# Other prices for float32 matmuls in a planned kernel, and constant matmuls in TensorE's planned gaps

## The chip, the cores and the metric

The kernel runs on one core of a Trainium2 chip. The metric is the device time of one execution in microseconds (us); less is better. Engines are called as in the profile: PE is TensorE (PEld its weight loads), DVE is VectorE, ACT is ScalarE, POOL is GpSimd, SP is SyncE, which here issues all DMAs.

## What is computed

An attention with random features, and behind it a feed-forward network (FFN) on its output, all in float32 to the outside:

```python
def phi(x):                                   # batch 8, heads 8, seq 576, head_dim 64, 128 features
    proj = np.einsum('bhsd,md->bhsm', x, omega)
    h = proj - np.sum(x * x, axis=-1, keepdims=True) / 2.0
    return np.exp(h - np.max(h, axis=-1, keepdims=True)) / np.sqrt(m)
q_p, k_p = phi(q * scale), phi(k * scale)
kv = np.einsum('bhsm,bhsd->bhmd', k_p, v)
num = np.einsum('bhsm,bhmd->bhsd', q_p, kv)
den = np.einsum('bhsm,bhm->bhs', q_p, np.sum(k_p, axis=2))[..., None] + 1e-06
x = (num / den).transpose(0, 2, 1, 3).reshape(4608, 512)
h = x @ w_in                                  # 512 x 2048
out = np.maximum(0.01 * h, h) @ w_out         # 2048 x 512
```

## The kernel before

The 4608 tokens are taken in nine blocks j of 512. For each block the attention is worked out for four pairs of heads (hp), and then the FFN of that block runs on PE. Key batches (`key_batch`, eight of them) deliver the sums over keys that a block needs; `query_block` does a block's queries. Batches 0 and 1 of the keys and block 0 of the queries are done in float32 (`Whole`): the projection at L636 (16 matmuls for four tiles of tokens, 4 more for a fifth tile), the sums over keys at L739, the transposes at L827 (`turn`) and the products with the sums at L856 (`num32`). All others (`Unit`) split each operand into two f16 parts: L572 projects, L751 to L753 sum over keys, L849 to L851 are the products. A block's products, divided (L866, L867, L869), are its x; x is split into f16 parts (`turned_parts`) and transposed by a DMA at L784 into the tiles `fix_xt`, on which the FFN works.

The FFN multiplies f16 parts in groups of 12 matmuls: L1210 up and L1234 down, with 512 columns, in the first blocks; L1126 and L1056, with 256 columns, where Strassen-like products are used. Block 0 has 16 groups up and 16 down. The weights arrive as eight pieces each of w_in and w_out (`fix_big`, SP L429 and L431), are converted (ACT L444 and L462, DVE L446, L449, L467, POOL L464), get the column sums of L457 on PE, and are split (L491, L335 and ACT L329) once their largest sum is known.

Nothing of this runs in the order in which it is written. Each step is an operation with one or more engines, a price in us for each, what it reads and writes, and a priority. `Plan.order` goes through time with these prices, gives each operation an engine and a start, gives each buffer a place, and so fixes the order on every engine, SP's queue included; then the operations are issued in that order, and each engine runs its own in order. FFN groups have the last priority, so they fill what the attention leaves of PE. `HOP` is the planned delay between an operation and its followers on other engines. The prices that the change touches are `PJ32` (0.5 us for a tile of tokens at L636), 10 x 0.235 at L739, 4 x 0.28 at L827 and 4 x 0.26 at L856.

PSUM, while the attention runs: three banks `ffn` (one of which first holds the column sums of the weights), two tiles `pj` for projections, one bank `mi` for everything small, so each product at L856 or L849 waits until the one before it has been read by L869.

Of the kernel before, what the change touches and what calls it, by code (L numbers as in the profile page):

```python
# [17 lines left out]
P = 128  # L18
# [38 lines left out]

UP_FIELD = 202 << 23
OM_DOWN = 2.0 ** 38
PJ, PJ32 = 0.07, 0.5  # L60


class Buf:
# [10 lines left out]
class Plan:  # L74
# [49 lines left out]
    def order(self):  # L124
# [44 lines left out]
        while len(done) < len(self.ops):  # L169
# [24 lines left out]
            for b in o.bufs:  # L194
                if b.place is None:
                    fs, us = place_free[b.kind], place_user[b.kind]
                    b.place = min((i for i in range(len(us)) if us[i] is None and (i < first_late[b.kind] or not early_left)),
                                  key=lambda i: fs[i])
                    us[b.place] = b
                    b.last, held_by[b.kind, b.place] = held_by.get((b.kind, b.place)), b  # L200
                    next_buf[b.kind] += 1
            o.start, o.engine = t, e
# [21 lines left out]
            for x in after[o.number]:  # L224
                x.waits -= 1
                x.ready = max(x.ready, t + o.cost if e == "PE" and "PE" in x.ways else end)
                if not x.waits:
                    open_.append(x)
        return done


def key_tiles(b):
# [26 lines left out]
def performer_ffn(ctx: ExitStack, tc, qT, kT, qn, kn, vn, omT, eye, w_in, w_out, out):  # L259
# [55 lines left out]
    def op(engine, cost, run, port=False, **of):  # L315
        return ways([(engine, cost, run, port or engine == "POOL")], **of)
# [393 lines left out]
    def key_batch(b, prio):  # L710
# [6 lines left out]
        for hp in range(HP):  # L717
# [14 lines left out]
            if b < WHOLE:  # L732
                def sums(u=u, edge=edge, acc=acc, hp=hp, parts=parts):
                    for j in range(2):
                        o = at(acc)[:, (2 * (hp % 2) + j) * E:(2 * (hp % 2) + j + 1) * E]
                        for t in range(VT):
                            c = t - b % 2
                            p = u.p()[:, 4 * j + c] if 0 <= c < 4 else edge32(edge)[:, j]
                            nc.tensor.matmul(o, p, parts()[:, hp, t, j], start=(t == 0), stop=(t == VT - 1))  # L739
                op("PE", 10 * 0.235, sums, r=[u.ph, edge, (v, 0), (v, 1)], w=[acc], prio=prio,  # L740
                   slack=1.0)
            else:
                def sums(u=u, edge=edge, acc=acc, hp=hp, parts=parts):
# [62 lines left out]
    def query_block(j, prio):  # L806

        for hp in range(HP):
# [6 lines left out]
            if j:  # L815

                for i in range(2):
                    op("SP", 1.25, lambda u=u, qp=qp, i=i: nc.sync.dma_start(out=at(qp)[:, i],
                       in_=flat(at(u.ph)[:, i]), transpose=True), r=[(u.ph, i)], w=[(qp, i)], prio=prio, moved=1 << 18)
            else:  # L820
                qp32 = lambda qp=qp: at(qp).rearrange("p a b t -> p (a b t)").bitcast(F32)
                for i in range(2):
                    turned = buf("ffn")

                    def turn(u=u, turned=turned, i=i):
                        for g in range(4):
                            nc.tensor.transpose(at(turned)[:, g * P:(g + 1) * P], u.p()[:, 4 * (g % 2) + 2 * i + g // 2, :],  # L827
                                                ident)
                    op("PE", 4 * 0.28, turn, r=[u.ph, "ident"], w=[turned], prio=prio)
                    high(512, lambda qp32=qp32, i=i: qp32()[:, 512 * i:512 * i + 512], lambda turned=turned: at(turned),  # L830
                         psum=True, r=[turned], w=[(qp, i)], prio=prio)
            strassen = j >= FIRST_S
# [2 lines left out]
            for i in range(2):  # L835
# [22 lines left out]
                if j:  # L858
                    op("PE", 12 * 0.035 + 0.1, num, r=[(qp, 0), (qp, 1), *((kvs[b], hp | 1) for b in used)], w=[acc],
                       prio=prio, slack=1.0)  # L860
                else:
                    op("PE", 4 * 0.26, num32, r=[(qp, i), (kvs["32"], hp | 1)], w=[acc], prio=prio)
                av = lambda acc=acc: at(acc)[:, :4 * E].rearrange("p (g e) -> p g e", e=E)

                def inverse(av=av, r=r, down=down):
# [399 lines left out]
    for j in range(NB):  # L1265
# [6 lines left out]
        if j + 1 < NB:  # L1272
# [3 lines left out]
                parts.append(key_batch(done_k, 0.0))  # L1276
            in_turn(*parts, query_block(j + 1, 0.0))
    order = plan.order()
    tiles.update({**opened(attention, "att", early, False), **opened(attention, "attps", early_banks, True)})
    ctx.push(attention)  # L1280
    opened_late = False
    with tc.manual_schedule():
        for o in order:
            if not opened_late and any(b.place >= len(tiles[b.kind]) for b in o.bufs):
                later()
                opened_late = True
            o.run()


# [45 lines left out]
```

## Time and profile before

| | us |
|---|---|
| median of 3 runs (lowest, highest) | 948.97 (947.88, 950.0) |
| the profiled execution | 958.32 |
| its span, from first to last instruction | 956.5 |
| busy: PE, DVE, ACT, POOL | 904.8, 707.7, 587.0, 419.7 |
| mean granted clock of PE | 0.967 |
| first FFN matmul (L1210) | 90.05 |

The lines are read so: a row of a stretch or a group gives busy time and, behind x, the number of instructions; idle time stands with what ended it. A float32 matmul of the program shows as two matmuls in the profile for L636, L739, L856 and L360, and as one for L827. PE's busy time holds the overlap of pipelined matmuls, so the price of one is read from the distance of starts.

### The profile page before, as it was taken

Reading aid. Unit: us, or ns where it says so; the run is one execution under the profiler, and the core shown is the slowest. Engines: PE = TensorE matmul, PEld = TensorE weight load, DVE = VectorE, ACT = ScalarE, POOL = GpSimd, SP = SyncE. Lnnn points to the kernel's source line nnn. Section 1 sums busy time; section 2 is a strip of 40 time slices with the busy share of each in tenths; the row PEclk is TensorE's granted clock in tenths of the full one; section 3 lists DMA queues with packets and bytes.
Section 4 is the critical chain, followed back from the end, with each engine's and each line's share of the span. In section 5 each row is a group of like instructions: output and inputs, shape, how many; then the busy total and the mean of one; then the engine's idle time right before and its main releaser. Section 6 shows DMA issues by size and latency. Waiting matters only on the chain.

```text
span 956.5 us, 20558 instructions
## 1 busy us (share of the span) xinstructions
PE 904.8 (95%) x8286; PEld 598.0 (63%) x8286; DVE 707.7 (74%) x1266; ACT 587.0 (61%) x874; POOL 419.7 (44%) x381
## 2 busy tenths in 40 slices
PE   4786999999999999998999999998998999999998
PEld 3785464645555545587557855784576647855887
DVE  7888987897899852887888777877786721285774
ACT  5777686557774763687747865786466723632661
POOL 2333541446665764336223640355025631555562
PEclk7786999999999999999999999999999999999999
DMA  9774446675587667898868995788779962751401
GB/s 368 256 210 126 142 112 148 149 159 121 99 137 186 138 166 175 172 199 226 219 142 186 238 243 126 180 201 187 159 123 209 227 123 82 201 130 40 133 1 45
DMA packets 260607, 155.07 MB, mean 162 GB/s; under 512 B 191648, under 2 KB 237472, under 8 KB 259488
## 3 DMA queue, kind: packets, MB, share of 16 engines
q1 hardware_dynamic: 260512, 153.76, 65.9%
q8 instruction: 65, 1.06, 0.5%
q14 instruction: 30, 0.25, 0.1%
HBM read 90.54 MB, written 16.78 MB: 112 GB/s over the span
## 4 chain that ended last, share of the span: by engine, by line
PE 79%; DMA 8%; DVE 8%; ACT 2%; issue 2%; SPq 1%; POOL 0%; DVEq 0%; ACTq 0%
PE fixps_ffn L1234 27%; PE fixps_ffn L1126 15%; PE fixps_ffn L1210 13%; DMA att_t<-att_z 5%; PE attps_pj L572 5%; PE lateps_ffn L1234 3%; PE attps_pj L636 3%; PE lateps_ffn L1056 3%; PE lateps_ffn L1126 2%; DMA att_qp<-att_ph 2%; PE fixps_ffn L1056 1%; PE attps_mi L849 1%; PE attps_mi L739 1%; DMA fix_xt<-fix_xn 1%; PE attps_mi L851 1%
## 5 line engine op out<-in xcount | busy, mean ns | idle before, releaser
L1234 PE MATMUL fixps_ffn<-fix_wt,fix_big 128*128 128x512 f16 x1392 | 314.3, 381 | 0.0
L1234 PEld LDWEIGHTS <-fix_big 128*128 128x128 f16 x1536 | 146.1, 98 | 168.2 <-issue 2.2
L335 POOL TENSOR_TENSOR fix_big<-fix_row,fix_big 128x512 f16<-128x512 f32 x131 | 162.3, 1246 | 201.4 <-ACT fix_big L329 191.4
L1126 PEld LDWEIGHTS <-fix_wt 128*128 128x128 f16 x2016 | 195.2, 98 | 29.7 <-issue 4.1
L1126 PE MATMUL fixps_ffn<-fix_xt,fix_wt 128*128 128x256 f16 x1800 | 208.1, 274 | 3.2 <-ACT fix_row L329 3.2
L1210 PE MATMUL fixps_ffn<-fix_xt,fix_wt 128*128 128x512 f16 x576 | 133.1, 386 | 2.1 <-DMA fix_xt<-fix_xn 2.1
L335 POOL TENSOR_TENSOR fix_xn<-fix_x,fix_xn 128x512 f16<-128x512 f32 (+1 forms) x36 | 42.3, 1174 | 129.7 <-ACT fix_xn L329 127.2
L1210 PEld LDWEIGHTS <-fix_wt 128*128 128x128 f16 x576 | 55.1, 99 | 66.5 <-issue 6.2
L591 ACT ACTIVATE att_p<-att_p,shift 128x1024 f32<-128x1024 f32 x68 | 69.7, 1028 | 40.4 <-DVE att_p L588 40.3
L329 ACT ACTIVATE fix_big<-fix_row 128x512 f16<-128x512 f32 x140 | 85.5, 623 | 10.6 <-DVE fix_wt L449 3.9
L579 DVE TENSOR_REDUCE att_st<-attps_pj 128x8 f32<-128x1024 f32 x68 | 72.8, 1076 | 19.3 <-PE attps_pj L572 19.3
L335 DVE TENSOR_TENSOR att_ph<-att_p,att_ph 128x1024 f16<-128x1024 f32 x56 | 75.6, 1355 | 10.4 <-ACT att_ph L329 10.3
L588 DVE SCALAR_TENSOR_TENSOR att_p<-attps_pj,att_sc,att_st 128x1024 f32<-128x1024 f32 x68 | 76.6, 1132 | 0.4
L1141 DVE TENSOR_TENSOR fix_row<-fix_row,fixps_ffn 128x512 f32<-128x512 f32 x64 | 43.9, 686 | 43.1 <-PE fixps_ffn L1126 21.7
L572 PE MATMUL attps_pj<-om,att_t 64*128 64x128 f16 x1416 | 51.1, 219 | 10.5 <-DMA att_t<-att_z 10.0
L329 ACT ACTIVATE att_ph<-att_p 128x1024 f16<-128x1024 f32 x55 | 57.5, 1047 | 1.4 <-PE attps_mi L753 1.1
L572 PEld LDWEIGHTS <-att_t 64*128 64x128 f16 x1416 | 40.5, 95 | 28.1 <-issue 14.1
L530 ACT ACTIVATE att_z<-att_nat 128x512 f32<-128x512 f32 (+1 forms) x56 | 36.2, 647 | 32.3 <-DMA att_t<-att_z 22.4
L532 DVE TENSOR_REDUCE att_sq<-att_z 128x8 f32<-128x512 f32 (+1 forms) x56 | 39.7, 708 | 21.4 <-ACT att_z L530 21.3
L1149 ACT ACTIVATE fix_row<-fix_row 128x512 f32<-128x512 f32 x70 | 43.5, 624 | 12.8 <-DVE fix_row L1141 12.4
L329 ACT ACTIVATE att_z<-att_nat,att_sc 128x512 f16<-128x512 f32 (+1 forms) x52 | 38.3, 739 | 21.0 <-DVE att_sc L542 21.0
L556 DVE SCALAR_TENSOR_TENSOR att_z<-att_nat,att_sc,att_z 128x512 f16<-128x512 f32 (+1 forms) x52 | 48.8, 941 | 3.2 <-ACT att_z L329 3.2
(185 smaller groups left out, 1584.4 us busy)
## 6 DMA issues: line engine op xcount, KB each, us to landing
fix_wt<-w1s SPq DMA_DIRECT2D x48, 512.0 KB, 4.7
fix_wt<-w1s SPq DMA_DIRECT2D x48, 384.0 KB, 3.9
att_v<-vn SPq DMA_DIRECT2D x16, 650.0 KB, 5.0
out<-fix_row SPq DMA_DIRECT2D x35, 256.0 KB, 2.3
fix_big<-w_in SPq DMA_DIRECT2D x8, 1024.0 KB, 10.1
fix_big<-w_out SPq DMA_DIRECT2D x8, 1024.0 KB, 5.4
att_nat<-qn SPq DMA_DIRECT2D x32, 256.0 KB, 3.3
w1s<-fix_y SPq DMA_DIRECT2D x32, 128.0 KB, 2.9
```

Source lines behind the costliest of these rows:

```text
L329: ("ACT", act(n, int(pointer)), lambda: nc.scalar.activation(dst(), src(), AF.Copy, scale=1.0 if scale is None else value()), False),
L335: return ways([(e, c, lambda g=g: g.tensor_tensor(dst(), a(), b(), op=ALU.subtract), True) for e, c, g in (("POOL", pool_(n), nc.gpsimd), ...
L556: op("DVE", stt(n) + 0.15, lambda: nc.vector.scalar_tensor_tensor(zl(), heads(), up(), zh(), op0=ALU.mult, op1=ALU.subtract), port=True, r ...
L572: nc.tensor.matmul(at(pj)[:, 512 * h + c * M:512 * h + (c + 1) * M], at(self.t)[r, 2 * (c0 + c) + x, :], om[r, w, :], start=(x + w == 0), ...
L579: op("DVE", dve(n * M), lambda: nc.vector.tensor_reduce(row(0), pv(), axis=AX.X, op=ALU.max), r=[pj], w=[st], prio=prio)
L588: op("DVE", dve(n * M), lambda: nc.vector.scalar_tensor_tensor(p(), pv(), down(), row(2).rearrange("p (g o) -> p g o", o=1).broadcast_to([ ...
L591: op("ACT", act(n * M, 1), lambda: nc.scalar.activation(flat(p()), flat(p()), AF.Exp, bias=shift), w=[p32], r=["ones"], prio=prio)
L1126: nc.tensor.matmul(o, unit(at(wb[c]), u)[:, wp, P * a:P * a + P], mixes[j, c][n][1](xp), start=(first and a == 0 and i == 0), stop=(a == 1 ...
L1141: op("DVE", dve(512), lambda: nc.vector.tensor_tensor(at(g), at(g), at(b), op=ALU.add), r=[b], w=[g], prio=top - 1.0)
L1149: op("ACT", act(512), lambda: nc.scalar.activation(at(g), at(src), AF.Prelu, scale=H_DOWN_D if finish else H_DOWN_S, alpha=0.01), r=[src], ...
L1210: nc.tensor.matmul(at(ph), wk[wp][:, c:c + P], xt[:, xp, :], start=(i == 0), stop=(i == 3 * KT - 1))
L1234: nc.tensor.matmul(at(po), part(f, gp)[:, t * P:(t + 1) * P], wf[wp], start=(f == 0 and gp == wp), stop=(f == FT - 1 and gp == 1))
```

## The change

Four prices of the planner are changed. And a function `between` goes through the order once it is fixed: wherever PE's next operation is planned at least 0.4 us behind the end of the one before, and one of the next 12 operations of PE is the first to write a `pj` or `ffn` buffer whose place is free by then, it notes a number of matmuls for that place, so many as take 0.8 of the gap at 256 columns / 2350 per us. When the kernel is issued, `busy` puts these in: `ident` (the 128x128 identity in float32, read as f16) is weight and operand, and the result goes into the PSUM place that the later operation will write over.

```diff
-PJ, PJ32 = 0.07, 0.5
+PJ, PJ32 = 0.07, 0.43
+FILL_FROM, FILL_LESS, FILL_SHARE, FILL_N = 0.4, 0.1, 0.8, 256
...
+                    b.free_at = fs[b.place]
...
+def between(order):
+    place = {o: i for i, o in enumerate(order)}
+    pe = [o for o in order if o.engine == "PE"]
+    first = [next((b for b in o.bufs if b.kind in ("pj", "ffn") and b.ops[0] is o), None) for o in pe]
+    fill, end = {}, pe[0].start + pe[0].cost
+    for i, o in enumerate(pe[1:], 1):
+        begin, gap = end, o.start - end
+        end = o.start + o.cost
+        if gap < FILL_FROM:
+            continue
+        for x, b in zip(pe[i:i + 12], first[i:i + 12]):
+            if b is None or (b.last and any(place[y] > place[o] for y in b.last.ops)):
+                continue
+            n = int((o.start - max(begin, b.free_at) - FILL_LESS) * FILL_SHARE / (FILL_N / 2350))
+            if n > 0:
+                fill[o] = b, n
+                break
+    return fill
...
-                op("PE", 10 * 0.235, sums, r=[u.ph, edge, (v, 0), (v, 1)], w=[acc], prio=prio,
+                op("PE", 10 * 0.118, sums, r=[u.ph, edge, (v, 0), (v, 1)], w=[acc], prio=prio,
...
-                    op("PE", 4 * 0.28, turn, r=[u.ph, "ident"], w=[turned], prio=prio)
+                    op("PE", 4 * 0.115, turn, r=[u.ph, "ident"], w=[turned], prio=prio)
...
-                    op("PE", 4 * 0.26, num32, r=[(qp, i), (kvs["32"], hp | 1)], w=[acc], prio=prio)
+                    op("PE", 4 * 0.118, num32, r=[(qp, i), (kvs["32"], hp | 1)], w=[acc], prio=prio)
...
     order = plan.order()
+    fill = between(order)
+    constant = ident.bitcast(F16)
+
+    def busy(b, n):
+        for _ in range(n):
+            nc.tensor.matmul(at(b)[:, :FILL_N], constant[:, :P], constant[:, :FILL_N], start=True, stop=True,
+                             skip_group_check=True)
...
+            if o in fill:
+                busy(*fill[o])
             o.run()
```

Lines of the changed kernel lie lower in the file by 25 from the projections on: L636 becomes L661, L739 L764, L827 L852, L856 L881, L457 L482, L1210 L1235, L615 L640, L429 L454. The fill is L1310. There are 412 fill matmuls, each with a weight load, in 30 runs of 2 to 40. Of them 321, in 24 runs, stand ahead of the first FFN matmul: 78 of these ahead of the first projection (in runs of 38, 35 and 5), the last ones in runs of 26, 15, 3 and 40. Three runs of 31, 24 and 17, and one of 2, stand where the first FFN block gives way to the second; runs of 6 and 11 come later.

Because the prices changed, all of the order is new. Three places show it. First, SP's queue at the start, where `fix_big` takes the pieces of w_in and `att_nat` the keys. Before:

```order
L380 DMA fix_xt_98<-omT 128x256
L381 DMA ident<-eye 128x128
L615 DMA att_nat_159<-kT 128x640
L429 DMA fix_big_88<-w_in 128x2048
L429 DMA fix_big_89<-w_in 128x2048
L429 DMA fix_big_90<-w_in 128x2048
L429 DMA fix_big_91<-w_in 128x2048
L670 DMA att_v_175<-vn 128x1300 x2
L615 DMA att_nat_160<-kT 128x640
```

And SP's queue at the same place in the changed kernel:

```order
L405 DMA fix_xt_98<-omT 128x256
L406 DMA ident<-eye 128x128
L454 DMA fix_big_88<-w_in 128x2048
L454 DMA fix_big_89<-w_in 128x2048
L454 DMA fix_big_90<-w_in 128x2048
L454 DMA fix_big_91<-w_in 128x2048
L640 DMA att_nat_159<-kT 128x640
L695 DMA att_v_175<-vn 128x1300 x2
L640 DMA att_nat_160<-kT 128x640
```

The first keys moved behind four pieces of w_in of 1 MB each. Second, DVE behind the splitting of omega, where `att_st`, `att_ph` and `att_edge` belong to the features of the first keys and `fix_wt` to the weights. Before:

```order
L643 TENSOR_REDUCE att_st_177<-attps_pj_201 128x8
L446 TENSOR_SCALAR fix_wt_65<-fix_wt_64 128x1024
L645 TENSOR_TENSOR att_ph_166<-attps_pj_201,att_st_177 128x1024
L449 SCALAR_TENSOR_TENSOR fix_wt_65<-fix_big_88,fix_wt_65 128x1024
L446 TENSOR_SCALAR fix_wt_67<-fix_wt_66 128x1024
L643 TENSOR_REDUCE att_st_178<-attps_pj_202 128x2
L645 TENSOR_TENSOR att_edge_168<-attps_pj_202,att_st_178 128x256
L446 TENSOR_SCALAR fix_wt_69<-fix_wt_68 128x1024
L449 SCALAR_TENSOR_TENSOR fix_wt_67<-fix_big_89,fix_wt_67 128x1024
```

And DVE at the same place in the changed kernel:

```order
L471 TENSOR_SCALAR fix_wt_65<-fix_wt_64 128x1024
L474 SCALAR_TENSOR_TENSOR fix_wt_65<-fix_big_88,fix_wt_65 128x1024
L471 TENSOR_SCALAR fix_wt_67<-fix_wt_66 128x1024
L471 TENSOR_SCALAR fix_wt_69<-fix_wt_68 128x1024
L474 SCALAR_TENSOR_TENSOR fix_wt_67<-fix_big_89,fix_wt_67 128x1024
L474 SCALAR_TENSOR_TENSOR fix_wt_69<-fix_big_90,fix_wt_69 128x1024
L471 TENSOR_SCALAR fix_wt_71<-fix_wt_70 128x1024
L699 TENSOR_REDUCE mx_v_128<-att_v_175 128x1 x2
L474 SCALAR_TENSOR_TENSOR fix_wt_71<-fix_big_91,fix_wt_71 128x1024
L668 TENSOR_REDUCE att_st_177<-attps_pj_201 128x8
```

The first features moved behind the conversion of four pieces of weights and the largest values of v. Third, PE behind the last transposes of block 0's queries, up to the first projection of key batch 1. Before:

```order
L856 MATMUL attps_mi_203<-fix_kv_81,att_qp_173 128x65 x4
L827 MATMUL fixps_ffn_113<-ident,att_ph_167 128x128 x4
L856 MATMUL attps_mi_203<-fix_kv_81,att_qp_174 128x65 x8
L636 MATMUL attps_pj_201<-fix_xt_98,att_nat_159 128x128 x2
L636 MATMUL attps_pj_201<-fix_xt_98,att_z_161 128x128 x2
```

And PE at the same place in the changed kernel, where the fill's rows that repeat are left out:

```order
L852 MATMUL fixps_ffn_113<-ident,att_ph_167 128x128 x4
L1310 LDWEIGHTS ident
L1310 MATMUL attps_pj_201<-ident 128x256
...
L881 MATMUL attps_mi_203<-fix_kv_81,att_qp_174 128x65 x4
...
L661 MATMUL attps_pj_201<-fix_xt_98,att_nat_159 128x128 x2
L661 MATMUL attps_pj_201<-fix_xt_98,att_z_161 128x128 x2
```

Fill matmuls, 7 ahead of the last product but one, 26 between the two, and 15 behind the last, now stand between the transposes, the products and the projection. At the end of the first FFN block PE had, before, the last two products of block 1 four and two groups ahead of that block's end; they now stand behind its 32nd group, with the run of 31 between them and the run of 24 behind them.

## The prediction

> **What bounds the kernel now.** I read the page first, then a table of stretches, then the waits of VectorE (DVE) and TensorE (PE), and last the chain of work and the order in time of the first 100 us.
>
> ```profile
> span 956.5 us, 20558 instructions
> PE 904.8 (95%) x8286; PEld 598.0 (63%) x8286; DVE 707.7 (74%) x1266; ACT 587.0 (61%) x874; POOL 419.7 (44%) x381
> PEclk7786999999999999999999999999999999999999
> ```
>
> PE is busy for 95% of the span, and the granted clock is low in the first four slices only, that is up to 96 us. The stretches (start and end, length, busy us of PE, PEld, DVE, ACT and POOL, granted clock, DMA share, GB/s) show what goes with it.
>
> ```profile
> 12.00:32.00 20.00, 10.82 (x107) 9.62 (x108) 16.85 (x25) 13.60 (x15) 8.46 (x8) 0.51 1.02 417
> 56.00:72.00 16.00, 13.99 (x158) 12.97 (x154) 14.43 (x23) 15.05 (x20) 1.23 (x1) 0.97 0.54 148
> 74.00:87.00 13.00, 8.67 (x52) 7.99 (x53) 10.29 (x18) 11.26 (x14) 4.89 (x3) 0.50 0.30 83
> 96.00:210.00 114.00, 109.62 (x901) 61.06 (x900) 98.11 (x160) 74.80 (x103) 48.49 (x44) 0.98 0.60 143
> 210.00:408.00 198.00, 198.00 (x1661) 101.02 (x1661) 150.25 (x291) 124.11 (x184) 114.23 (x102) 0.99 0.67 148
> 408.00:780.00 372.00, 358.05 (x3766) 249.00 (x3765) 288.82 (x573) 248.80 (x383) 148.26 (x150) 0.99 0.84 190
> ```
>
> In the head PE is granted half a clock where it is busy for little more than half of the time (12 to 32, 74 to 87) and a full one where it is busy (56 to 72). From 210 to 408 PE never idles; from 408 to 780 it idles 14 us. In the head DVE is the busiest engine, and this is what it waits for there (sum, times, longest):
>
> ```profile
> DVE att_st L643 <- PE attps_pj L636: 7.6, 4, 2.9
> DVE pow_w L364 <- PE attps_mi L856: 1.4, 1, 1.4
> DVE pow_v L364 <- PE attps_mi L360: 0.8, 1, 0.8
> DVE att_r L866 <- PE attps_mi L856: 0.6, 2, 0.3
> ```
>
> So a faster PE is worth something in the head alone, and there at most these waits and the cold matmuls at the start of the FFN. The pieces of the chain of work (start, length, what) give the price of a matmul at either clock; L636 is one projection, L739 one sum over keys, L856 one product with the sums, L1210, L1126 and L1234 groups of 12 FFN matmuls.
>
> ```profile
> 64.88 1.99 PE attps_pj L636 x32
> 66.87 2.39 PE attps_mi L739 x20
> 82.18 1.97 PE attps_mi L856 x8
> 84.15 3.69 PE attps_pj L636 x32
> 89.97 0.37 SPq L527
> 90.43 3.81 DMA fix_xt<-fix_xn
> 95.70 3.76 PE fixps_ffn L1210 x12
> 99.65 2.61 PE fixps_ffn L1210 x12
> 141.42 2.18 PE attps_mi L739 x20
> 882.62 1.31 PE fixps_ffn L1126 x12
> ```
>
> A projection takes 1.99 warm and 3.69 cold; a group of 512 columns 2.61 and up to 3.76.
>
> **The prices.** The planner now takes 4 x 0.43 = 1.72 for a projection, 10 x 0.118 = 1.18 for L739 and 4 x 0.118 = 0.47 for L856. The trace has 1.99 and 2.18 for the first two, and for L856 and L827 at a clock of 1.00, by the distance of their starts:
>
> ```profile
> 42.25 1.11 PE L856 MATMUL attps_mi<-fix_kv,att_qp 128*128 128x65 f32 x8
> 43.29 1.09 PE L827 MATMUL fixps_ffn<-ident,att_ph 128*128 128x128 f32 x8
> 44.22 0.34 PE L457 MATMUL fixps_ffn<-ones,fix_wt 128*128 128x1 bf16 x8
> ```
>
> L856 takes 1.04, where the old price was 1.04; eight transposes of L827 take 0.93, that is 0.46 for four, as the new price says. So of the four new prices one is right (L827), one is 14% short, and two are half of what the trace has at full clock. Gaps that stand behind an L739 or an L856 are therefore planned 1.0 or 0.57 us too long, and the fill, 0.8 of the gap, takes up what is left of them.
>
> **The fill.** One of its matmuls has the shape of L1126 (128x128 weights, 256 columns, f16): 1.31 / 12 = 0.109 us at full clock, twice that at half. 412 are 45 us; 321 stand ahead of the first FFN matmul (35.0 us), 91 behind it. Each brings a weight load:
>
> ```profile
> L1126 PEld LDWEIGHTS <-fix_wt 128*128 128x128 f16 x2016 | 195.2, 98 | 29.7 <-issue 4.1
> ```
>
> The loads of L1126 take 98 ns each, and 12 matmuls with 12 loads still take 1.31, so I count the loads at nothing: the matmul before covers them. The Trainium skill, TensorE: Matmul & The Clock Gate, Part 3 (The mechanism), says that a weight load overlaps a running matmul only where the row groups differ, which a fill's full 128 rows do not; its Part 2 allows it into a background buffer. By the first a fill would cost 98 + 109 = 207 ns; the row above speaks against that.
>
> **Part 1, the start.** SyncE's (SP) queue now sends four w_in pieces ahead of the first kT. The rows of the start, SP's issues and the ACT instructions that waited for them:
>
> ```profile
> 1.67 0.42 SPq L615 DMA_DIRECT2D att_nat<-kT  x1
> 2.13 2.04 SPq L429 DMA_DIRECT2D fix_big<-w_in  x4
> 4.97 0.74 ACT L616 ACTIVATE att_z<-att_nat 128x640 f32<-128x640 f32 x1 [2.96 <-DMA att_nat<-kT]
> ```
>
> Four pieces are 4.19 MB; at the 417 GB/s of the row of 12 to 32 they take 10.1 us. kT then lands near 4.97 + 10.1 = 15.0, its square is done at 15.8, and the first projection starts at about 16 instead of 5.0. The 78 fill matmuls ahead of it (8.5 us warm, up to 17 cold, from 4.6 on) end by then or slightly late. DVE, which began its first features at 9.17, instead starts on the weights, which land 2.5 us apart for 1.9 us of its work: about 3.7 us of new idling. The bytes up to 32 us are the same, so the weights themselves are not later.
>
> **Part 2, PE up to the FFN.** From 16 on PE has, at full clock: 10 projections x 1.99 = 19.9, 4 of a quarter's size 2.0, 4 L739 x 2.3 = 9.2, 8 L856 x 1.04 = 8.3, 4 x 0.93 for L827 = 3.7, 9 column sums x 0.3 = 2.7, two L360 0.6: 46.4 us. The 243 remaining fill matmuls add 26.5. Without a single wait the first FFN group starts at 16 + 72.9 = 88.9. Before, the third group started at 99.65; two groups at full clock (5.2) and a column sum (0.2) earlier is 94.2, which I take as the start to compare with (cold matmuls are in it). So the head can gain 5.3 at most, and each us that PE has to wait in it comes off, since the fill leaves no slack.
>
> Does DVE allow 88.9? The rows that count:
>
> ```profile
> 77.85 1.28 DVE L491 SCALAR_TENSOR_TENSOR fix_wt<-fix_wt,pow_w,fix_wt 128x1024 f16<-128x1024 f32 x1
> 82.05 1.22 DVE L449 SCALAR_TENSOR_TENSOR fix_wt<-fix_big,fix_wt 128x1024 uint32<-128x1024 uint32 x1
> 83.18 0.69 DVE L446 TENSOR_SCALAR fix_wt<-fix_wt 128x1024 uint32<-128x1024 uint32 x1
> 84.60 0.42 DVE L869 TENSOR_TENSOR fix_x<-attps_mi,att_r 128x256 f32<-128x256 f32 x1
> 87.89 1.22 DVE L643 TENSOR_REDUCE att_st<-attps_pj 128x8 f32<-128x1024 f32 x1 [2.87 <-PE attps_pj L636]
> ```
>
> The last piece of x for the first FFN (the eighth L869) ends at 85.0. The new order puts two L446, one L449 and one L491 behind it (3.9 us); of the waits for PE ahead of it (7.6 - 2.9 for L636, 1.4 and 0.8 for L364, 0.6 for L866: 7.5) I take 5.4 as gone and the rest as kept, since PE has the fill to do at those places; 3.7 come at the start. 85.0 - 3.9 - 5.4 + 3.7 = 79.4. Behind it stand 15 fill matmuls, two projections, 3 and 40 fill matmuls: 1.6 + 4.0 + 0.3 + 4.4. SP's transposing DMA of the last x waits, before as now, for the second of these projections (the row at 89.97), so 3.81 us later it is there while the 40 still run. (On POOL its low part now goes ahead of one sign product; SP's wait covers either.) DVE and PE so agree on 89 to 91. I take 1.2 us of waits: the FFN starts at 90.1, 4.1 earlier.
>
> **Part 3, the first FFN block and its end.** Its 32 groups (32 x 2.59 = 82.9) stand before and now among the attention of the next block, but in the new order the features of that block's last head pair (L572) come behind 26 groups instead of 21, and the last two products (L849 to L851) behind all 32, with 31 fill matmuls between them. Before, the last product stood two groups ahead of the block's end:
>
> ```profile
> 200.54 0.19 PE L849 MATMUL attps_mi<-fix_kv,att_qp 128*128 128x65 f16 x1
> 204.41 2.75 PE L1234 MATMUL fixps_ffn<-fix_wt,fix_big 128*128 128x512 f16 x12
> 205.13 1.35 SPq L784 DMA_TRANSPOSE fix_xt<-fix_xn  x1
> 209.12 0.84 PE L572 MATMUL attps_pj<-om,att_t 64*128 64x128 f16 x24 [1.97 <-DMA att_t<-att_z]
> 209.90 7.04 PE L1210 MATMUL fixps_ffn<-fix_xt,fix_wt 128*128 128x512 f16 x24
> ```
>
> From that product to the issue of its transposed x took 4.6, and the transfer 3.81: 8.4. Those two groups covered it; now nothing does. New sum: 90.1 + 82.9 + other PE work (4 L739 x 2.18, 6 L572 x 0.84, 2 L636 x 2.0, 7 column sums x 0.3, 6 products x 0.5, rest 0.8: 23.6) + waits 0.8 = 197.4; + product 0.6 + 31 fills 3.4 + 8.4 = 209.8. So of the 4.1 us nearly all is stalled away, and the second block starts at 209.8 instead of 209.90. One thing stays: the 24 matmuls at 209.90 took 6.9 to the next start where two groups take 5.2, the clock having dropped in the wait; the 24 + 17 + 2 fills there keep it up: -1.7. Gain so far 1.8.
>
> **Part 4, the rest.** From 210 to 408 PE is saturated and the new order puts the attention at nearly the same groups, so the 1.8 is carried. Later the attention stands up to 24 us of FFN work earlier; its 14 us of PE's idle time from 408 to 780 may be dealt out anew. I know no sign for that: 0, with bounds of -5 and +5 (a third of the 14 either way). The last 17 fill matmuls (1.9 us) stand in planned gaps: 0, at worst +1.9.
>
> Sum: 958.32 - 1.8 = 956.5 for a profiled execution. That one is 9.35 above the median of the runs, as profiling costs something throughout; I take the same 1.8 off the median: 948.97 - 1.8 = 947.2.
>
> **Rivals.** A difference below 0.2%, 1.9 us, can hardly be told from none here.
> - The head's gain is kept. For it: DVE is ahead by some 4 us and is no longer behind PE; if the products are not late, the 31 fills end in DVE's own wait, and the 3.4 is no extra. Then 5.3 + 1.7, less 1, some 6: 943.
> - Slower, by the fill in the head. PE is in order, and two of the prices that size the gaps are half of the measured ones. Each us that PE waits for DVE, ACT or SP between 16 us and the first FFN group moves all that follows, while the fill stays. With 3 us of waits the gain is nil, from 5 on it is slower than 0.2%, with 8 the FFN starts at 96.9 and the end comes 5 later: 954. Against it: the sum on DVE's side comes out no later.
> - Nothing moves: what the head gains the block's end takes in full, and with its waits the clock drops as before: 949.
> - The weight load is not covered: 243 x 0.098 = 23.8 later, 969. The trace's L1126 row all but excludes it.
>
> **How the numbers follow.** Forecast (from -5 to +1.5 us, 944 to 950.5) 0.42; gain kept 0.24; slower by the fill 0.22; nothing moves 0.10; uncovered loads 0.02. The forecast's own range lies half beyond -1.9, four tenths within, one tenth at the slow end with Part 4's bounds. Faster: 0.21 + 0.24 = 0.45. Same: 0.17 + 0.10 = 0.27. Slower: 0.04 + 0.22 + 0.02 = 0.28. The range reaches to the rival that is faster with its share of Part 4 (943 - 5) and to the slower one at 954 with 1 more: 938 to 955.
>
> **What would show it.** Right: a granted clock near 1.0 from about 10 us to 96; the first projection near 16; L739 still 2.2 and L856 1.04; the first L1210 group (L1235 there) between 89 and 92; a wait of PE between the last product and the second block. Wrong: PE waits of over 3 us in sum between 16 and 90; a clock that stays at 0.5 among fills; fills more than 0.12 us apart; or a PE idle sum from 408 to 780 that is far from 14 us, which would put the outcome down to the order of later work and not to the head.

## The result and the profile after

The changed kernel is slower. It took 958.53 us (median; 957.92 to 967.62) beside 951.48 for the kernel before on the same chip: ratio 1.0096, 95% interval 1.0068 to 1.0124. A second set of runs gave 1.0093 (1.0061 to 1.0125). The forecast was 947.2, range 938 to 955. Runs of one kernel spread by up to 0.9% around their median, so below ratios are compared, and spans only where both profiles of the changed kernel show the same thing.

The first two lines come from the page of the changed kernel, the others from its table of stretches (start and end, length, busy us of PE, PEld, DVE, ACT and POOL, granted clock, DMA share, GB/s).

```profile
span 965.8 us, 21368 instructions
PEclk9999999989999999999899999999999999999999
```

```profile
12.00:32.00 20.00, 17.61 (x194) 14.49 (x193) 19.83 (x24) 12.63 (x13) 6.82 (x8) 0.91 1.02 415
56.00:72.00 16.00, 15.79 (x171) 14.39 (x170) 13.08 (x20) 12.27 (x16) 1.16 (x1) 1.00 0.51 138
74.00:87.00 13.00, 13.00 (x152) 12.22 (x149) 12.30 (x21) 12.41 (x16) 2.73 (x2) 1.00 0.13 26
96.00:210.00 114.00, 111.16 (x922) 64.17 (x921) 94.64 (x155) 73.44 (x100) 55.84 (x49) 1.00 0.60 141
210.00:220.00 10.00, 5.44 (x59) 3.88 (x60) 9.90 (x12) 3.94 (x6) 4.40 (x4) 0.66 0.52 122
210.00:408.00 198.00, 189.32 (x1677) 99.64 (x1678) 161.99 (x304) 124.36 (x185) 111.14 (x103) 0.97 0.71 152
408.00:780.00 372.00, 363.79 (x3751) 251.99 (x3750) 279.18 (x559) 246.97 (x378) 137.79 (x139) 0.99 0.81 185
```

The clock in the head is 0.91 (12 to 32) and 1.00 (74 to 87) where it was 0.51 and 0.50. Not all of that is the fill: without it, the new order has 0.83 and 0.75 there (e1 below). But from 210 to 408, where PE never idled before, it now idles 8.7 us, 4.6 of them between 210 and 220, where DVE is busy for 9.90 of 10. There the first FFN block gives way to the second. PE in that place, in order of time (start, us, and in brackets the idle time ahead and what ended it):

```profile
202.30 3.55 PE L1310 MATMUL fixps_ffn<-ident 128*128 128x256 f16 x31
206.06 0.19 PE L874 MATMUL attps_mi<-fix_kv,att_qp 128*128 128x65 f16 x1 [0.22 <-DVE fix_x L894]
...
206.43 2.78 PE L1310 MATMUL fixps_ffn<-ident 128*128 128x256 f16 x24
...
215.18 3.79 PE L1310 MATMUL attps_pj<-ident 128*128 128x256 f16 x17 [4.56 <-DVE att_p L613]
218.89 0.95 PE L597 MATMUL attps_pj<-om,att_t 64*128 64x128 f16 x24
219.78 0.39 PE L1310 MATMUL fixps_ffn<-ident 128*128 128x256 f16 x2
220.01 2.75 PE L1235 MATMUL fixps_ffn<-fix_xt,fix_wt 128*128 128x512 f16 x12
```

The second block starts at 220.0 instead of 209.9 (220.5 in the profile of the second set). SyncE's queue at the same place:

```profile
211.49 0.37 SPq L552 DMA_DIRECT2D att_nat<-kn  x1
211.95 1.58 SPq L583 DMA_TRANSPOSE att_t<-att_z  x1
213.63 1.28 SPq L809 DMA_TRANSPOSE fix_xt<-fix_xn  x1
```

And DVE, on which both wait: L552 needs the buffer that L581 reads, and the 17 fill matmuls need the `pj` tile that L613 reads.

```profile
207.04 0.42 DVE L894 TENSOR_TENSOR fix_x<-attps_mi,att_r 128x256 f32<-128x256 f32 x1
207.38 1.22 DVE L360 TENSOR_TENSOR att_ph<-att_p,att_ph 128x1024 f16<-128x1024 f32 x1
...
209.82 1.64 DVE L581 SCALAR_TENSOR_TENSOR att_z<-att_nat,att_sc,att_z 128x512 f16<-128x512 f32 x1
...
213.84 1.67 DVE L613 SCALAR_TENSOR_TENSOR att_p<-attps_pj,att_sc,att_st 128x1024 f32<-128x1024 f32 x2
```

Before, the same pair of L588 started at 204.53. So DVE is 9 us late here, and it is the bound from about 207 on. Yet it had idled shortly before. Busy times from 150 to 200, of the kernel before and of the changed one (DVE is the third of the engines), and what DVE waited for from 160 to 210, in the changed kernel (first two rows) and before (last two):

```profile
150.00:200.00 50.00, 47.96 (x415) 26.40 (x414) 40.91 (x72) 28.73 (x36) 17.29 (x14) 0.97 0.60 134
```

```profile
150.00:200.00 50.00, 50.00 (x438) 29.63 (x438) 38.20 (x76) 32.17 (x41) 22.52 (x19) 1.00 0.69 138
```

```profile
DVE att_sq L557 <- ACT att_z L555: 3.7, 2, 3.1
DVE att_r L891 <- PE attps_mi L876: 3.3, 5, 1.4
DVE att_sq L532 <- ACT att_z L530: 3.2, 1, 3.2
DVE att_r L866 <- PE attps_mi L851: 1.4, 1, 1.4
```

PE is saturated there, and DVE waits five times, 3.3 us in all, for products of PE that stand behind FFN groups in PE's queue; before, it waited once, 1.4. The larger wait, for ACT, is nearly the same in both. These waits are only a part of the 9 us. The whole way up to the pair of L588 and of L613 shows the rest:

```profile
0.00:204.53 204.53, 173.18 (x1491) 118.94 (x1492) 173.30 (x282) 137.74 (x176) 74.88 (x63) 0.87 0.63 187
0.00:213.84 213.84, 200.81 (x1878) 141.90 (x1879) 178.81 (x285) 141.10 (x179) 90.80 (x73) 0.99 0.63 186
```

Up to this step DVE has idled 3.8 us more than before, and has been busy 5.5 us longer, with only three instructions more. In the second profile it is busy 6.4 us longer. So more than half of the lateness is in DVE's instructions ahead of this step (three more, and others that last longer), not in waits. Why they last longer isn't shown. (In the same time POOL has been busy for 90.8 us instead of 74.9.)

The FFN of block 0 is done early (201.9 instead of 207.2); the attention of block 1, which the second block needs, is late, and then PE waits.

To add this up I use one more measure, worked out from all matmul starts of a trace. Each matmul but the fill is counted with its distance to the next one at full clock (0.216 us with 512 columns, 0.109 with 256, and so on, the same for all kernels). *Lag* is the time at which a given amount of this work has been started, less the work: idle time, fill and cold matmuls together. At 55 us of work the head is over, the end of block 0's FFN stands near 150, and at 170 the second block is under way.

| lag, us, at work of | 55 | 150 | 170 |
|---|---|---|---|
| before | 47.7 | 52.1 | 55.8 |
| changed | 46.4 | 48.5 | 64.2 |
| changed, second profile | 47.1 | 48.9 | 64.7 |

The changed kernel is 3.2 to 3.6 us ahead at the end of the first block and 8.4 to 8.9 behind after the change of blocks. That is the loss; from there on the two profiles of the changed kernel gain 23.1 and 17.2 of lag and the one of before 22.2, a difference of no clear sign.

### The profile page after: what moved, and what is told of

Same layout as the page of the kernel before. It is cut to its first block, busy times and chain, and to the rows that moved or that the text cites. A ratio compares the mean times of both kernels' runs of the same rounds, so it can differ in the third digit from the quotient of the medians.

```text
span 965.8 us, 21368 instructions
## 1 busy us (share of the span) xinstructions
PE 934.7 (97%) x8698; PEld 625.1 (65%) x8698; DVE 710.3 (74%) x1269; ACT 586.8 (61%) x872; POOL 419.2 (43%) x380
## 4 chain that ended last, share of the span: by engine, by line
PE 84%; DMA 8%; DVE 5%; ACT 2%; issue 1%; SPq 0%; DVEq 0%; ACTq 0%
PE fixps_ffn L1259 31%; PE fixps_ffn L1151 17%; PE fixps_ffn L1235 10%; PE attps_pj L597 5%; DMA att_t<-att_z 4%; PE lateps_ffn L1259 3%; PE lateps_ffn L1081 3%; PE lateps_ffn L1151 2%; PE attps_pj L661 2%; PE attps_mi L764 2%; DMA att_qp<-att_ph 1%; PE fixps_ffn L1310 1%; PE attps_mi L874 1%; PE fixps_ffn L1081 1%; DMA fix_big<-w_in 1%
## 5 line engine op out<-in xcount | busy, mean ns | idle before, releaser
L1151 PE MATMUL fixps_ffn<-fix_xt,fix_wt 128*128 128x256 f16 x1800 | 205.4, 274 | 1.2 <-ACT fix_row L354 1.2
L1235 PE MATMUL fixps_ffn<-fix_xt,fix_wt 128*128 128x512 f16 x576 | 129.6, 379 | 2.7 <-ACT fix_row L1242 2.3
L1235 PEld LDWEIGHTS <-fix_wt 128*128 128x128 f16 x576 | 54.6, 98 | 65.8 <-issue 3.6
L360 POOL TENSOR_TENSOR fix_xn<-fix_x,fix_xn 128x512 f16<-128x512 f32 (+1 forms) x36 | 39.8, 1105 | 101.1 <-ACT fix_xn L354 100.8
L613 DVE SCALAR_TENSOR_TENSOR att_p<-attps_pj,att_sc,att_st 128x1024 f32<-128x1024 f32 x68 | 76.6, 1133 | 0.5
L354 ACT ACTIVATE fix_row<-fixps_ffn 128x512 f32<-128x512 f32 x62 | 36.3, 592 | 28.0 <-PE fixps_ffn L1151 27.7
L581 DVE SCALAR_TENSOR_TENSOR att_z<-att_nat,att_sc,att_z 128x512 f16<-128x512 f32 (+1 forms) x52 | 47.3, 910 | 1.6 <-ACT att_z L354 1.4
```

Source lines behind the costliest of these rows:

```text
L354: ("ACT", act(n, int(pointer)), lambda: nc.scalar.activation(dst(), src(), AF.Copy, scale=1.0 if scale is None else value()), False),
L360: return ways([(e, c, lambda g=g: g.tensor_tensor(dst(), a(), b(), op=ALU.subtract), True) for e, c, g in (("POOL", pool_(n), nc.gpsimd), ...
L581: op("DVE", stt(n) + 0.15, lambda: nc.vector.scalar_tensor_tensor(zl(), heads(), up(), zh(), op0=ALU.mult, op1=ALU.subtract), port=True, r ...
L613: op("DVE", dve(n * M), lambda: nc.vector.scalar_tensor_tensor(p(), pv(), down(), row(2).rearrange("p (g o) -> p g o", o=1).broadcast_to([ ...
L1151: nc.tensor.matmul(o, unit(at(wb[c]), u)[:, wp, P * a:P * a + P], mixes[j, c][n][1](xp), start=(first and a == 0 and i == 0), stop=(a == 1 ...
L1235: nc.tensor.matmul(at(ph), wk[wp][:, c:c + P], xt[:, xp, :], start=(i == 0), stop=(i == 3 * KT - 1))
```

## The experiments

Ratios are against the kernel before on the same chip. "Changed" stands for the kernel with all four new prices and the fill (1.0096).

**The order or the fill?** Four kernels, told apart by which prices make the order and which fill is in it.

e1, the new order without fill:

```diff
-    fill = between(order)
+    fill = {}
```

> The changed kernel without any of its 412 fill matmuls: the new order of all engines alone. Theory A (the order: block 1's last products stand behind the whole of FFN block 0, so the second FFN block waits for attention): still slower than the kernel before, 954 to 961 us, with the second FFN block starting 5 us or more later than the 209.9 of before, and PE idle for 8 us or more between the end of the first FFN block and the second; TensorE cold in the head (clock 0.5 to 0.8) and the first FFN group 1 to 3 us later than the 92.6 of the changed kernel. Theory B (the fill itself costs the time: matmuls that PE runs while what it should do waits): equal to the kernel before or faster, 943 to 952.

966.4 us, ratio 1.0175 (1.0125 to 1.0225), above what either theory gave. The order by itself loses, and more than expected; in this order the fill is no cause of the loss but takes back 0.8%. Lag 60.2, 60.4, 76.0 at 55, 150 and 170: without the fill the head is 14 us worse, and the change of blocks costs 15.6 as in the changed kernel (15.7).

```profile
12.00:32.00 20.00, 13.03 (x129) 11.57 (x129) 19.86 (x24) 12.63 (x13) 6.69 (x8) 0.83 1.01 415
...
74.00:87.00 13.00, 8.77 (x56) 8.00 (x55) 10.07 (x18) 9.80 (x13) 1.15 (x1) 0.75 0.35 119
```

e2, the four old prices with `between` as it is: 240 fill matmuls, only 9 of them at the change of blocks.

> The four old prices, so the old order, with the fill put into its planned gaps (240 matmuls, 185 of them ahead of the last 32 in front of the first FFN group, 9 at the end of the first FFN block). Theory A: the second block starts no later than before, the head gains 0 to 4 us by the clock: 946 to 952. Theory B: slower than before, 954 or more, since the fill is there.

950.14, ratio 0.9992 (0.9965 to 1.0019): no difference, as theory A had it. The head gains 5.6 us of lag (42.1 at 55), and 55.3 at 170 leaves 0.5 of them.

e3, the changed kernel with only the fill ahead of the first FFN operation:

```diff
     for i, o in enumerate(pe[1:], 1):
+        if o.filler:
+            break
```

> The changed kernel without the fill from the first FFN matmul on (321 less the 40 just ahead of it stay; the 31, 24, 17 and 2 at the end of the first FFN block, and the 6 and 11 later, are gone). Theory A: of the 10 us by which the second block starts late, 2.9 are the run of 17 in a bank that VectorE releases late; without it PE is cold for two groups (+1.7): 955 to 959. Theory B: all of the loss is these runs, 947 to 951.

959.6, ratio 1.0086 (1.0053 to 1.0119), 0.1% from the changed kernel and just above theory A's range; the 40 ahead of the first group are gone too, which makes the head 2 us worse (48.5 at 55). The runs of 31, 24 and 17 are not the loss: without them the second block starts at 217.3, 2.7 earlier, and the lag at 170 is 63.4.

e4, the prices that the trace has at full clock:

```diff
-PJ, PJ32 = 0.07, 0.43
+PJ, PJ32 = 0.07, 0.4975
-                op("PE", 10 * 0.118, sums, ...
+                op("PE", 10 * 0.218, sums, ...
-                    op("PE", 4 * 0.118, num32, ...
+                    op("PE", 4 * 0.26, num32, ...
```

> Prices as the trace measures them at full clock (0.4975 for a tile of L661, 10 x 0.218 for L764, 4 x 0.115 for the transposes, 4 x 0.26 for L881), with the fill (325 matmuls). Theory A: the order made of these prices also puts the last product behind 31 or 32 groups of the first FFN block and 35 fills behind it, so it loses there as the changed kernel does: 955 to 963. Theory C (the two wrong prices, half of what the trace has, are why the order is bad): 945 to 951.

948.53, ratio 0.9979 (0.9951 to 1.0007). Theory A in its general form falls: here, too, the last product stands behind the block's end, and it costs little. Lag 41.2, 42.4, 49.1: the change of blocks takes 6.7, not 15.7. So the prices were next.

e5, as e4 without fill; e6, as e4 with the fill up to the first FFN group only.

> The order made of the measured prices (as in e4), without any fill. If the fill pays in the head whatever the order (it took 15 us off the lag of the changed order by the end of the first block): 954 to 960, with the clock of the head back at 0.5 to 0.8. If it was the better order alone that brought e4 back to the time of before: 947 to 950.

> As e4 (measured prices), with the 276 fill matmuls up to the first FFN group and without the 49 at the end of the first FFN block. If those 49 hold nothing back (the second block waits for its x meanwhile) and keep the clock up: 949 to 951, up to 2 us slower than e4's 948.5. If they hold PE for late banks as the run of 17 does in the changed kernel: 943 to 947.

e5: 953.42, ratio 1.0018 (0.9991 to 1.0044), just under its first range: this order without fill is where before was, and the fill is worth 0.4% (e4) to 0.66% (e6). e6: 947.5, ratio 0.9952 (0.9928 to 0.9976), between its two ranges; the interval overlaps that of e4, so the 49 matmuls at the end of the block are worth nothing that can be measured.

**The queues at the change of blocks.** e8 moves four steps of the changed kernel by hand and leaves out the fill behind the first FFN group:

```diff
...
     fill = between(order)
+    by = {o.number: o for o in order}
+    for one, other in ((652, 854), (653, 854), (654, 811), (658, 811)):
+        order.remove(by[one])
+        order.insert(order.index(by[other]), by[one])
```

> The changed kernel with the fill up to the first FFN group only (the 91 behind it left out, as in e3, but the 40 just ahead of the first group stay), and with four steps moved by hand at the end of the first FFN block: the low part of the last x on POOL ahead of one weight product, its transposing DMA on SP's queue ahead of one load of keys (which waits for VectorE) and of one transposed att_z, and the first two FFN groups of the second block ahead of the projection L597 on PE. If SP's in-order queue and the order on PE hold the second block: it starts near 213.5 instead of 217.3 (e3) and 220.0 (changed kernel), and the time is 953 to 957. If the x itself comes too late (VectorE's chain): it starts at 216 or later and the time is 958 to 960, as e3.

956.89, ratio 1.0062 (1.0036 to 1.0088), at the slow end of the first range. In this kernel lines lie one lower (L810 is L809).

```profile
209.76 1.23 SPq L810 DMA_TRANSPOSE fix_xt<-fix_xn  x1
211.60 0.38 SPq L553 DMA_DIRECT2D att_nat<-kn  x1
```

```profile
PE attps_mi L875 <- DVE fix_x L895: 3.6, 1, 3.6
PE attps_mi L779 <- DVE att_edge L361: 2.7, 2, 2.3
```

The DMA is issued 3.9 earlier and the second block starts at 210.9, 9 us earlier than in the changed kernel and even earlier than expected; the time falls by 0.3%, about 3 us (0.2% against e3, which also has no fill there; the intervals overlap), and the lag at 170 is still 63.9. PE gets its two groups sooner, but it waits for DVE's `fix_x` ahead of them and for `att_edge` behind them. One reason why the gain is small is the clock (0.80 from 210 to 220, 0.71 from 220 to 230): without the fill the first groups of the second block run partly cold, 24 matmuls in 6.84 and 7.75 us where two groups take 5.2 at full clock.

```profile
210.94 6.84 PE L1236 MATMUL fixps_ffn<-fix_xt,fix_wt 128*128 128x512 f16 x24
226.15 7.75 PE L1236 MATMUL fixps_ffn<-fix_xt,fix_wt 128*128 128x512 f16 x24
```

So these moves alone don't bring the time back. The waits named in the first traces (SP's order, the run of 17) are where the lateness shows; behind them DVE is late. The same moves with the fill kept were not run.

**Which price?** e7 mends the two halved prices in the changed kernel (L764 10 x 0.218, L881 4 x 0.26; the projection stays 14% short), e12 that of L764 alone. e10 and e11 try one consequence of the shorter prices: an operation's priority is an offset less 1/10000 of the planned time from it to the end, and the shorter path puts the first keys' load just behind four loads of w_in. e10 sets it right in the changed kernel by the offset alone; e11 does the reverse in the kernel before, without fill.

```diff
 LATER = {"s": 0.0, "w1": -15.0, "w2": -275.0,
-         "k": -5.0, "q": -565.0, "m": 0.0}
+         "k": -6.4, "q": -565.0, "m": 0.0}        # e10; e11 has -4.0
```

> Only the two prices that are half of the measured ones are mended (L764 10 x 0.218, L881 4 x 0.26); the projection stays at 0.43 for a tile, which is 14% short; fill in the gaps (378). If the wrong prices make the bad order: 946 to 952, as e4. If the order jumps with any small difference of a price, good or bad: its second block stands 4 us later in the plan than e4's, and then 954 to 962.

> The changed kernel once more, for a second profile and more runs: 957 to 960 (its profiled run at 967.6 was the slowest of seven). What both profiles show is the kernel's, what only the first shows (a second block at 220.0, idle time of 4 us between 220 and 418) may be that run's.

> The changed kernel with one number changed, the offset of the key batches' priority (-5.0 to -6.4), so that the first keys' load goes ahead of the four pieces of w_in again (its priority comes out 0.000005 before theirs); prices and fill rule stay, 436 fill matmuls. Theory D (the place of the first keys' load in SP's queue, which the lower prices tipped, makes the bad order): first projection near 5, end of the head's lag as in e4 and e7, 944 to 951. Theory E (the half prices misplace work elsewhere too, here column sums of w_out ahead of the first FFN group): 953 to 960.

> The kernel before (old prices, no fill) with the same offset the other way (-5.0 to -4.0), so that the first keys' load goes behind the four pieces of w_in. Theory D: the first projection moves from 5 to 16 and the time to 956 to 966, near the 966 of the new order without fill. If that place costs nothing by itself: 948 to 952.

> The changed kernel with only the price of L764 mended (10 x 0.218; L881 stays at half of what the trace has, L661 at 0.43 for a tile), with fill (413). The first keys' load then still stands behind the four pieces of w_in, by 0.000035 of priority. Theory D: slow like the changed kernel, 955 to 962. Theory C (the wrong prices are the cause by themselves, L764's error being the largest): about half of the way back, 950 to 954.

e7: 946.97, ratio 0.9951 (0.9925 to 0.9978). e9, the second set of the changed kernel: 958.77. e10: 957.91, ratio 1.0073 (1.0043 to 1.0103), hardly better than changed, with a lag of 56.0 already in the head. e11: 958.48, ratio 1.0077 (1.0049 to 1.0104). e12: 947.56, ratio 0.9966 (0.9948 to 0.9984), with the keys still behind the weights. So theory D falls: late keys do harm in the old order (e11), but with them the kernel can be fast (e12) and without them slow (e10). e10's loss, though, has another place. Its FFN starts at 103.00 instead of 92.07 (ahead of it PE's column sums wait 5.0 us in all for DVE's weights), while from the end of the first block (210.1) to the second (219.3) it takes 9 us instead of 18. So e10 does not show that late keys have no part in what the changed kernel loses at the change of blocks. What e12 shows is that mending one price is enough.

**Is that a rule or chance?** e13 halves L764's price among the old ones, e14 among the measured ones, e15 puts the keys first in e12 (offset -6.4), e16 takes 10 x 0.327 for L764 among the measured prices. e17 mends in the changed kernel the projection alone, e18 L881 alone.

> The old prices with that of L764 alone halved (10 x 0.118), and the fill (371 matmuls); to be held against e2 (old prices, fill: 0.9992 of before). Theory F (L764 planned at half its time makes the order bad): 1.005 to 1.012 of before, 955 to 962. Theory G (no rule: each change deals out another order): anywhere from 0.995 to 1.012, and e13 and e14 need not agree.

> The measured prices of e4 with that of L764 alone halved (10 x 0.118), and the fill (368). To be held against e4 (0.9979). Theory F: 1.005 to 1.012, 955 to 962. Theory G: anywhere, 0.995 to 1.012.

> As e12 (L764's price mended, the others as changed), with the offset -6.4, so that the first keys' load goes ahead of the four pieces of w_in; fill 421. Theory F: L764's price is right, so the order is good: 0.993 to 0.999, 943 to 950. Theory G: anywhere; 1.004 or more would speak against F.

> The measured prices of e4 with that of L764 half as long again (10 x 0.327), and the fill (311). Theory F, if it is too short a price that harms: 0.993 to 1.000, 943 to 951. If any wrong price harms: 1.004 or more. Theory G: anywhere.

> The changed kernel with the projection's price mended (0.4975 for a tile), L764 and L881 both at half; fill 391. If the two halves together make the loss: 1.006 to 1.011, 956 to 961. If the short price of the projection is needed as well: 0.998 to 1.003, 949 to 954.

> The changed kernel with L881's price mended (4 x 0.26), L764 at half and the projection at 0.43 for a tile; fill 389. If the two halves together make the loss: 0.998 to 1.003, 949 to 954, as e13 and e14. If half of L764 and the short projection make it: 1.006 to 1.011, 956 to 961.

| L764's price, the rest | right or long | half |
|---|---|---|
| old prices, fill | e2 0.9992 | e13 1.0028 (1.0005 to 1.0051) |
| measured prices | e4 0.9979; e16, too long, 0.9942 (0.9918 to 0.9967) | e14 0.9999 (0.9971 to 1.0027) |
| projection short | e7 0.9951 | e18 1.0014 (0.9989 to 1.0039) |
| L881 half | not run | e17 1.0054 (1.0031 to 1.0077) |
| projection short, L881 half | e12 0.9966 | changed 1.0096, 1.0093 |
| the same, keys first | e15 0.9953 (0.9928 to 0.9979) | e10 1.0073 |

In all five rows that have both, half is slower, by 0.2 to 1.3% (with the old and with the measured prices the intervals overlap). Theory F has the sign; its size was wrong for e13 and e14, where the half price costs 0.2 to 0.4% and not 1. (e17 lies just under the range for "the two halves together", e18 within it.) The whole loss needs more than that price: the half price of L881 beside it adds 0.55% (e17 against e14) and 0.8% (changed against e18), the short projection 0.15% (e18 against e14) and 0.4% (changed against e17). A price that is too long did no harm in the one case that was run (e16, which with 945.55 us is the fastest kernel of all; e7, e6, e15 and e12 lie within its interval). Theory G isn't excluded for the small differences, but it gives no reason for the sign in five rows. With a price the fill changes too; only e1 and e5 hold it apart. Without any fill the order of the changed prices is at 1.0175 and that of the measured ones at 1.0018, so there the order alone makes the difference.

A rough sign in the trace goes with it. DVE's busy time from 150 to 200 is 37.2 to 39.9 of 50 in all kernels at 1.005 and above (e1, e3, e8, e10, e17, changed) but e11, whose loss arose in the head too, and 39.97 (e18) to 46.5 in the others. There is no gap between the two groups, and within the second the busy time doesn't follow the ratio (e13, at 1.0028, has 44.0), so it tells only the ends apart. First e16, then e17:

```profile
150.00:200.00 50.00, 49.56 (x462) 28.04 (x461) 46.46 (x84) 31.03 (x40) 29.28 (x23) 1.00 0.72 157
```

```profile
150.00:200.00 50.00, 50.00 (x427) 29.42 (x426) 38.37 (x70) 31.27 (x40) 18.10 (x17) 1.00 0.64 142
```

The lag at 170 is 49.1 (e4) to 58.3 (e12) in all kernels at or below 1, 56.2 and 59.2 in e13 and e5, 60.8 in e18, 61.4 (e17) to 64.7 (changed) in those from 1.005 to 1.010, and 76.0 in e1. That the slow order comes from these prices is shown by the runs; by which choices the planner gets from a price to late products was not followed step by step and stays open.

## Why the prediction was wrong, point by point

- **The prices**: read rightly, used too little. That L764 and L881 were planned at half of what the trace has was in the prediction, but its consequence was sought in the size of the fill alone. The consequence was the order (e7, e12).
- **Part 1**: right. First projection at 15.95 (16 predicted), in the second profile 16.3.
- **Part 2, DVE's 5.4 us**: the first term that failed. The last x of the head was put at 79.4, on the reckoning that 5.4 of DVE's 7.5 us of waits for PE would go.

```profile
83.26 0.42 DVE L894 TENSOR_TENSOR fix_x<-attps_mi,att_r 128x256 f32<-128x256 f32 x1
```

It began at 83.26, 1.3 earlier than before's 84.60. The waits moved to other places (12 to 92 us):

```profile
DVE att_st L668 <- PE attps_pj L661: 3.4, 5, 1.3
DVE att_r L891 <- PE attps_mi L881: 2.7, 5, 1.3
DVE att_ph L670 <- PE attps_mi L764: 1.9, 2, 1.3
DVE att_r L891 <- PE attps_mi L385: 1.2, 1, 1.2
```

They sum to 9.2, all of it ahead of that x, where before had 7.5 and the forecast left 2.1. In this order a PE at full clock was not there sooner when DVE needed it. (Nor is DVE the busiest engine in all of the head, as the prediction read its rows: from 56 to 72 and from 74 to 87 ACT is, with 15.05 and 11.26 us beside DVE's 14.43 and 10.29.) The FFN started at 92.07, and its third group at 97.97, which less 5.4 is 92.6: a gain of 1.6 and not 4.1.
- **The price of a fill matmul**: right. With no wait ahead, 40 of them take 92.07 - 87.71 = 4.36 us, 0.109 each, weight loads covered.

```profile
87.71 4.53 PE L1310 MATMUL fixps_ffn<-ident 128*128 128x256 f16 x40
92.07 2.11 PE L1235 MATMUL fixps_ffn<-fix_xt,fix_wt 128*128 128x512 f16 x9
94.53 3.40 PE L1235 MATMUL fixps_ffn<-fix_xt,fix_wt 128*128 128x512 f16 x15 [0.35 <-DMA fix_xt<-fix_xn]
```

At 98 ns more for an uncovered load they would have taken 8.3. The row agrees with Part 2 of the Trainium skill's TensorE: Matmul & The Clock Gate, which lets a load go ahead into the background buffer, and not with the reading of its Part 3 that was a rival.
- **Part 3, the end of the first block**: the step that failed. The place was right (products behind the block's end, PE waiting for x), the size was not: second block at 220.0 instead of 209.8. From the last product to the issue of its DMA took 213.63 - 206.06 = 7.6, not 4.6, since SP's queue was held by L552. The 31 fill matmuls, put at 3.4, cost nothing: behind them PE still waited 0.22 for DVE. The runs that were to keep the clock up (-1.7) did not: the 17 stood in a `pj` tile that DVE freed at 215.1, the clock was 0.66 from 210 to 220, and they ran cold ahead of the block (3.79 us); the block's groups behind them ran at full clock. But e8, where the second block starts 9 us sooner, is faster by only some 3 us. Missing altogether was the state of DVE: the sum had PE's work for 23.6 us of attention inside the block and never asked whether DVE would have finished it. The fill itself gave a hint beforehand: 74 matmuls of 0.109 at 0.8 of a gap are 10.1 us of planned idle time between the blocks, in an order whose prices were known to be too short; by the old prices it is 9 matmuls, 1.2 us (e2). It is no more than a hint: with the measured prices it is 49 matmuls, 6.7 us, and that kernel isn't slow (e4).
- **Part 4**: inside its ±5 (+0.9 and -5.0 by lag from 170 on, in the two profiles). PE's idle time from 408 to 780 was 8.2, where 14 stood as the mark. That profiling costs 9.35 us throughout, as the prediction had it, isn't borne out: the profiled executions of e4, e16 and e17 (946.94, 945.40, 958.16) are below their medians (948.53, 945.55, 958.41). Only the base of the sum hung on it.
- **The rivals**: "gain kept" and "nothing moves" assumed that DVE keeps up. "Slower, by the fill in the head" had the sign and half of the size (954 is 5 us more than before, 1.0096 is 9) for another reason: e1 and e3 show that in this order the fill in the head saves time. None of the signs of being wrong looked at DVE ahead of the second block.

## What to carry to other kernels

A planner that orders work by prices took an error on the short side worse than one on the long side here: with one price halved the kernel was slower in each of five plans (in two of them within the intervals), with it raised by half it was not in the one plan tried. Don't put a price that is known to be wrong down to its direct term alone: it deals out a new order. And judge an order by whether the engine that must feed the next stage will have done its work by then (here DVE), not by the waits in which its lateness shows; removing those waits moved the second block by 9 us and the end by 3.

## What the hardware showed

In this order, matmuls of a constant raised the granted clock from 0.83 to 0.91 (12 to 32 us) and from 0.75 to 1.00 (74 to 87; e1 against changed), and they started it too: in a run of 38 from 4.35 to 10.17 us some 15 ran at half pace (15 x 0.218 + 23 x 0.109 = 5.8), that is 3.3 us until the full clock came. The Trainium skill, TensorE: Matmul & The Clock Gate, Part 1, gives about 3.4 us of sustained work for it; the rows agree.

```profile
4.35 5.87 PE L1310 MATMUL fixps_ffn<-ident 128*128 128x256 f16 x38
10.17 0.35 PE L482 MATMUL fixps_ffn<-ones,fix_wt 128*128 128x1 bf16 x8
```

What the fill was worth depended on the order: 0.8% in the new one (e1 against changed), 0.4 to 0.7% with the measured prices (e5 against e4 and e6), and nothing that can be measured in the old one (e2), where the head's 5.6 us of lag were given back by the time the second block was under way.
